# Fourteen empty GpSimd instructions in front of each indirect transfer in place of eight, in a kernel whose order of work is planned anew for it

## The chip, the cores and the metric

The kernel runs on one core of one Trainium2 chip. What is measured is the device time of one execution in microseconds, from a median over runs; profiles are of single executions. TensorE (PE) does the matmuls, PEld is its weight load, VectorE is DVE, ScalarE is ACT, GpSimd is POOL, and SyncE (SP) issues the plain transfers.

## What is computed

Two layers, one behind the other. The first mixes 8 sequences of 2496 rows of 256 numbers in the frequency domain:

```
X = rfft(x, axis=1)
Yr = Xr @ w_r - Xi @ w_i + b_r ;  Yi = Xr @ w_i + Xi @ w_r + b_i
Y  = soft threshold of Yr and of Yi at 0.01
y  = irfft(Y)                                   # 19968 rows of 256
```

The second sends each of the 19968 rows to one of 8 experts. The scores are `y @ w_gate`; all row-expert pairs are walked from the highest score down, a row takes the first expert that has room, and each expert has room for 2496 rows. A row's result is `relu(row @ w1[e]) @ w2[e]`, with 1024 hidden units.

## The kernel before

**Stages.** The sequences are worked on one after the other (batch 0 to 7). Each goes through a transform over 39 points (11 pieces), a transform over 64 points with the weights and the soft threshold (10 units, "p"), its way back (T2, lines 1153 to 1165), and the inverse transform over 39 points (11 pieces, lines 1171 to 1211), after which the rows are stored to `YD`, transposed, split in three bf16 parts (lines 1211 to 1222) and multiplied with the gate; the scores are stored to `LG`. Products that need fp32 accuracy are made of a high and a low part, so most results leave PSUM twice, once by ACT (high part) and once by DVE or POOL (the remainder).

**Routing and experts.** After half of the batches an early round gives each expert 512 rows (8 jobs of 4 row tiles). Then eight closing rounds follow, one expert each. A closing round finds its threshold by a search: DVE counts (line 454), PE adds the counts over the partitions (lines 464 and 465), DVE decides (lines 482 to 486). Then PE, ACT and DVE make the list of rows (`lists`), and the expert takes the remaining 1984 rows in 16 tiles of 128.

**Indirect transfers.** Gathers of rows (line 640), of an expert's weights (line 617) and the scatter of results (line 702) are indirect transfers that POOL issues: 32 + 128 gathers of rows, 32 of weights, 160 scatters, 352 in all. All go through one helper, and `GAP` empty instructions stand ahead of each:

```
def ind(self, pos, emit, nbytes, reads, writes, run=1024, late=0.0, bare=False):
    g = Q['gb'] if bare else Q['gw']
    def spaced():
        for _ in range(GAP): self.P.engine_nop()
        return emit()
    return self.plan.add('P', g + 1.05, pos, spaced, reads, writes, load=moved(nbytes, run, g + 1.2, 1.4, late))
```

POOL also makes the remainders of the inverse transform's input (line 955) and, for some batches, the third part of the rows (line 1222).

**The order.** Nothing is ordered by hand. Each operation is given to a planner (`Plan`) with its engine, an assumed duration, a position and what it reads and writes. The planner plays the program through with these durations and writes each engine's instructions in the order in which it could start them, with the position as the tie-break. On the chip every engine then runs its own list strictly in that order and waits where an input is late. The numbers that steer it are `Q` (positions, spacings and a few assumed costs), `LATE` (how much later than computed transfers land: `sp` plain ones, `raw` weights, `gather`, `scatter`), `SLACK` (a reserve added when an input comes from another engine), and the sets of batches that choose the engine for an operation: `BV` (the bias is added by DVE at line 1126; for other batches PE adds it with one more matmul, line 1120), `SOFT` (the soft threshold's first step runs on ACT, line 1139; for others on DVE, line 1142), `YLV` (the third part of the rows is made by DVE; for others by POOL, both line 1222). `gb` and `gw` are the cost that the planner counts for the empty instructions, `gb` for the second gather into a buffer, `gw` for all other indirect transfers.

Of the kernel before, what the change touches and what calls it, by code (L numbers as in the profile page):

```python
# [273 lines left out]
        return max(t.end for t in self.tasks)  # L274


GAP = 8
REV = True
UX = 6
P1X = -7.47  # L280
LATE = dict(sp=1.71, raw=8.75, gather=1.87, scatter=6.24)
SLACK = dict(split=1.82, count=0.02, back=0.12, lists=0.47, os=0.66, hid=0.45, mm4=0.34, mm4l=0.17, tr=0, trl=0.67, gate=0, gatel=0.55)
IOTA = True
Q = dict(hV=0.094, hA=0, hT=0, hP=0.264, e0=55.111, e1=84, en=225.161, le=33.14, ge=20.432, c0=1023.643, cs=63.758, c1=1110.092, c1a=1127.294, n0=190.708, n2=98.843, ll=30.291, gs=26.531, gl=3.929, be=16.256, bl=61.604, xp=14.084, f0=7.351, p1=0.237, p1s=0.741, p57=2.721, p57s=0.545, p5=3.525, p56s=0.982, p5s=0.706, xl=0.922, xs=0.435, m2=-0.211, m3=0.7, zz=0.824, m4=1.256, l5=0.297, s5=-1.07, w5=0.141, t5=0.888, g5=1.134, r0=16.37, gb=0.407, gw=0.319, lg=0.185, aa=0.3, ba=0.243, sc=1.967, k2=2.026)
YLV = (0, 1, 5, 7)
SOFT = (2, 3, 4, 5)


def moved(nbytes, run, lead=1.6, back=1.8, late=0.0, k=16): return lead, nbytes / run * (0.009 + 3.68e-5 * run if run <= 4096 else 7e-5 * run) / k, back + late
# [21 lines left out]
class Kit:  # L311

    def __init__(self, tc, nc, ctx, rings, groups={}):
        self.tc, self.nc = tc, nc
        self.V, self.A, self.P, self.T = nc.vector, nc.scalar, nc.gpsimd, nc.tensor
        self.plan = Plan(rings, groups, hold=dict(V=Q['hV'], A=Q['hA'], T=Q['hT'], P=Q['hP']))
        self.sp = ctx.enter_context(tc.tile_pool(name="sb", bufs=1))
# [18 lines left out]

    def dma(self, pos, emit, nbytes, reads, writes, run=1024, late=0.0, **k): return self.plan.add('SP', 0.4, pos, emit, reads, writes, load=moved(nbytes, run, late=LATE['sp'] + late), **k)
# [8 lines that stand above are left out]
# [99 lines left out]
def count(K, H, pos, c, no, ag, cols, pk, junk, acc, eqs=[], nt=1):  # L445
# [17 lines left out]
    def mm():  # L463
        T.matmul(ps.t[:, 0:n], lhsT=H.ones, rhs=cn.t[:, 0:n], start=True, stop=True)
        if n2: T.matmul(ps.t[:, n:2 * n], lhsT=H.sml, rhs=cn.t[:, n:2 * n], start=True, stop=True)
    K.t(.15, p, mm, [cn, H.b_ones, H.b_sml], [ps], slack=SLACK['count'])
    return ps
# [54 lines left out]
def lists(K, H, pos, pre, ps2, cols, nt, iota, bs, pk, jl, gi, o, top, parts, group=None):  # L522
# [10 lines left out]
    ps3 = K.psum(pk, [128, cols + 1])  # L533
    K.t(.1, pos(), lambda: T.matmul(ps3.t, lhsT=H.dif, rhs=RD.t, start=True, stop=True), [RD, H.b_dif], [ps3], slack=SLACK['lists'])
    plan.add('A', .052 + cols / 1200, pos(), lambda: A.copy(RDd.t, ps3.t), [ps3], [RDd], slack=SLACK['lists'])
    SmP = []
# [7 lines left out]
    for a, b in parts:  # L544
        for t0 in range(a, b, per):
# [3 lines left out]
            def mm(t0=t0, n=n, pl3=pl3):  # L549
                for q in range(n):  # L550
                    T.matmul(pl3.t[:, q], lhsT=Sm.t[:, 128 * (t0 + q):128 * (t0 + q) + 128], rhs=RDd.t, start=True, stop=True)
            Sm.users.append(K.t(.09 * n, pos(), mm, [RDd] + SmP[t0:t0 + n], [pl3], slack=SLACK['lists']))
            d = done[t0] = plan.buf(None, None)
# [41 lines left out]
class Experts:  # L595
# [7 lines left out]
    def load(self, pos, e=None, wi=None):  # L603
# [3 lines left out]
        for k in range(2):  # L607
            for m in range(2):
# [7 lines left out]
                else:  # L616
                    K.ind(p, lambda r=r, k=k, m=m: K.P.indirect_dma_start(out=r.t, out_offset=None, in_=self.rows[k],
                                                                          in_offset=bass.IndirectOffsetOnAxis(ap=wi.t[:, m:m + 1], axis=0)), 524e3, [wi], [r], run=4096, late=LATE['raw'])

# [10 lines left out]
    def run(self, n, base, W, gi, go, gs, oi, oo, pos_g, early=False):  # L630
# [6 lines left out]
        for t in range(NT):  # L637
            if not t % 2: xg[t // 2] = K.sb("xg", [128, 2, 256])
            g = xg[t // 2]
            q = K.ind(pos_g(t), lambda t=t, g=g: P.indirect_dma_start(  # L640
                out=g.t[:, t % 2], out_offset=None, in_=self.YD[0:EB * S] if early else self.YD, in_offset=bass.IndirectOffsetOnAxis(ap=gi.t[:, go + t:go + t + 1], axis=0)),
                131e3, [gs[t]] + (self.YDb[0:EB] if early else self.YDb), [g], late=LATE['gather'], bare=t % 2 == 1)
            gi.users.append(q)

        def xpose(c, pos):
            nt = min(4, NT - 4 * c)
            xT[c] = [[K.sb("xT", [128, 512], F32R) for _ in range(2)] for _ in range(2)]
            for m in range(2):
                h, l = xT[c][m]
                ps = K.psum("psx", [128, 512])  # L650

                def tr(ps=ps, m=m):
                    for q in range(nt):
                        t = 4 * c + q
                        T.transpose(ps.t[:, 128 * q:128 * q + 128], xg[t // 2].t[:, t % 2, 128 * m:128 * m + 128], H.idn)  # L655
                K.t(.109 * nt, pos + .5 * m, tr, [H.b_idn] + [xg[t] for t in range(2 * c, 2 * c + (nt + 1) // 2)], [ps])
                w = 128 * nt
                plan.add('A', .052 + w / 1200, pos + .5 * m, lambda ps=ps, h=h: A.copy(h.t[:, 0:w], ps.t[:, 0:w]), [ps], [h])
                v(w, pos + .5 * m, lambda ps=ps, h=h, l=l: V.tensor_tensor(l.t[:, 0:w], ps.t[:, 0:w], h.t[:, 0:w], op=OP.subtract), [ps, h], [l])

        def ffn1(c, ft, pos):
            w = min(512, n - 512 * c)
            hh, hl = K.sb("hid", [128, 512], F32R), K.sb("hid", [128, 512], F32R)
            hT[c, ft] = (hh, hl)
            ps = K.psum("psh", [128, 512])

            def mm(m):
                h, l = xT[c][m]
                for q, (a, x_) in enumerate(((0, h), (0, l), (1, h))):
                    T.matmul(ps.t[:, 0:w], lhsT=W1[m].t[:, a, 128 * ft:128 * ft + 128], rhs=x_.t[:, 0:w], start=q + m == 0, stop=q + m == 3)  # L670
            for m in range(2):
                K.t(3 * (.004 + .000446 * w), pos + .5 * m, lambda m=m: mm(m), [W1[m]] + xT[c][m], [ps])
            hi = plan.buf(None, None)
            plan.add('A', .052 + w / 1200, pos, lambda: A.activation(hh.t[:, 0:w], ps.t[:, 0:w], AF.Relu), [ps], [hh, hi])
            e = w - n % 128 if c == NC - 1 else w
            if e < w: v(w - e, pos, lambda: V.scalar_tensor_tensor(hh.t[:, w:2 * w - e], ps.t[:, e:w], 0.0, hh.t[:, e:w], op0=OP.max, op1=OP.subtract), [ps, hi], [hh])
            v(e, pos, lambda: V.scalar_tensor_tensor(hl.t[:, 0:e], ps.t[:, 0:e], 0.0, hh.t[:, 0:e], op0=OP.max, op1=OP.subtract), [ps, hi], [hl])

        def ffn2(c, q, pos):
# [21 lines left out]
            def sc():  # L701
# [3 lines left out]
                self.scat.append(ins)  # L705
            K.ind(pos + Q['sc'], sc, 131e3, [o, oi], [], late=LATE['scatter'])

        HD, k = 2, base
        xpose(0, base - Q['xp'])
        for ft in range(HD): ffn1(0, ft, base - Q['f0'] + ft)  # L710
        for c in range(NC):
# [8 lines left out]
            for q in sorted(range(min(4, NT - 4 * c)), reverse=REV and not early and c == NC - 1):  # L720
                ffn2(c, q, k)
                k += Q['k2']

# [177 lines left out]


PLAIN1, PLAIN5 = (), (7,)
BV = (0, 1, 2, 3, 4)
BANKS = [f"b{i}" for i in range(7)] + ["pt0"]
QUOTA = dict(p1=2, p5=2, ps2=2, ps3=2, pa=1, ps4=2, pT=2, pL=1, psh=3, pl=1, pso=2, psx=1, pq=1)
LATER = ('psh', 'pl', 'pso', 'psx', 'pq')
# [2 lines left out]
def phase_a(K, H, x, w_r, w_i, b_r, b_i, w_gate, cD1, cF, cG, cD5, YD, LG, NB=B):  # L910
# [26 lines left out]
    def act(n, ps=True): return (0.052 if ps else 0.095) + n / 1200  # L937
    def dve(n): return 0.068 + n / 960
# [3 lines left out]
    def add_dma(pos, emit, nbytes, reads=(), writes=(), eng='SP', after=(), run=1024, k=16, late=None):  # L942
        return plan.add(eng, 1.05 if eng == 'P' else 0.4, pos, emit, reads, writes, after=after, load=moved(nbytes, run, *((1.2, 1.4) if eng == 'P' else ()), late=LATE['sp'] if late is None else late, k=k))

# [84 lines left out]
    def batch(b):  # L1029
# [66 lines left out]
        for p in range(10):  # L1096
# [19 lines left out]

            pb = b not in BV

# [18 lines left out]
            plan.add('V', dve(512), pos + Q['zz'], lambda pc=pc, sx=sx, y=y: V.tensor_tensor(y.t, pc.t, sx.t[:, None, :].to_broadcast([128, 2, 256]), op=OP.add), [pc, sa], [y], uses=[sx])  # L1137
            if b in SOFT:
                plan.add('A', act(512, False), pos + Q['zz'], lambda y=y, t=t: A.activation(t.t, y.t, AF.Relu, bias=mlam, scale=1.0), [y, Bml], [t])
# [362 lines left out]
```

## Time and profile before

| | |
|---|---|
| Time, median of 3 runs | 1576.14 us (1571.86 to 1578.77) |
| The profiled execution's own time | 1571.82 us |
| Its span, from the first to the last instruction | 1570.0 us |
| Mean granted TensorE clock | 0.987 of full speed |
| PE busy | 1496.4 us (95%) |
| DVE busy | 1209.5 us (77%) |
| ACT busy | 883.9 us (56%) |
| POOL busy | 515.0 us (33%) |

The span begins with 47 us in which the first data arrive. To about 556 us the transforms run, with the early round's lists from about 380 us on; the last batch's scores and the experts' early jobs follow to about 790 us, and then the closing rounds' experts to the end. Busy shares are means over these stages. Matmuls are pipelined and overlap in the records, so what one more matmul costs is read from when the next ones start.

### The profile page before, as it was taken

The numbers are of one execution on the slowest core, as the hardware profiler recorded it, in microseconds if no ns is written. First come the engines' busy times: TensorE is split into PE (matmuls) and PEld (weight loads), VectorE is DVE, ScalarE is ACT, GpSimd is POOL, SyncE is SP. The second block draws the span as 40 slices with busy tenths as digits, with TensorE's granted clock in tenths as the row PEclk, the third lists the DMA queues.
The fourth block names the chain that finished last, engine by engine and source line by source line (L and its number), as shares of the span: only waits on it lengthen the run. The fifth ranks groups of instructions, "written<-read, shape, count | busy, mean of one in ns | idle before, by whom it ended". The sixth has DMA issues, their size and how long they took to land.

```text
span 1570.0 us, 31267 instructions
## 1 busy us (share of the span) xinstructions
PE 1496.4 (95%) x9391; PEld 1245.5 (79%) x9398; DVE 1209.5 (77%) x3999; ACT 883.9 (56%) x2060; POOL 515.0 (33%) x486
## 2 busy tenths in 40 slices
PE   6999999999999899998999999898999999999997
PEld 4888888888788758887787887787887878878886
DVE  5889887778999877998899997897787765563432
ACT  2778999998798854445435253344353442652331
POOL 0012215244353623114415224225233252454111
PEclk8999999999999999999999999999999999999999
DMA  9787888887788574332213122122111221231000
GB/s 323 217 275 250 245 267 273 232 268 210 239 252 251 171 206 136 110 112 92 81 44 95 33 75 63 33 76 70 63 61 52 78 70 54 92 96 61 22 24 28
DMA packets 138387, 212.07 MB, mean 135 GB/s; under 512 B 27188, under 2 KB 99553, under 8 KB 138209
## 3 DMA queue, kind: packets, MB, share of 16 engines
q1 hardware_dynamic: 118239, 151.66, 30.9%
q0 software_dynamic: 19840, 58.22, 11.7%
q8 instruction: 76, 1.25, 0.3%
q14 instruction: 102, 0.84, 0.2%
q10 hardware_dynamic: 130, 0.11, 0.0%
HBM read 125.18 MB, written 84.75 MB: 134 GB/s over the span
## 4 chain that ended last, share of the span: by engine, by line
PE 75%; DVE 13%; ACT 5%; DMA 3%; issue 2%; POOL 1%; another core or an unknown queue 1%; SPq 0%; POOLq 0%; ACTq 0%; DVEq 0%
PE b L670 21%; PE b L689 14%; PE b L690 7%; PE b L1124 6%; PE b L1153 4%; PE b L1105 3%; PE pt L670 3%; PE b L1132 3%; DVE junk L454 3%; PE b L1191 3%; PE b L1067 2%; PE pt L689 2%; PE b L655 1%; PE b L1211 1%; PE pt L690 1%
## 5 line engine op out<-in xcount | busy, mean ns | idle before, releaser
L955 POOL TENSOR_TENSOR s2l<-s2c,s2h 120x512 fp32r<-120x512 f32 (+1 forms) x84 | 105.7, 1265 | 272.4 <-ACT s2h L952 231.0
L454 DVE SCALAR_TENSOR_TENSOR junk<-h_m,st,h_AG 128x156 bf16<-128x156 f32 (+1 forms) x472 | 160.4, 382 | 2.2
L702 POOL DMA_INDIRECT out_dram<-xTh,li x64 | 65.4, 1022 | 273.4 <-DVE xTh L699 154.5
L1124 PE MATMUL b<-wt,xTh 128*128 128x256 f32 x640 | 126.6, 295 | 0.0
L1124 PEld LDWEIGHTS b<-wt,xTh 128*128 128x128 f32 x640 | 102.7, 191 | 7.5 <-issue 2.9
L1105 PE MATMUL b<-FG,sh 128*128 128x128 f32 x640 | 89.2, 281 | 12.7 <-DMA sh<-T 12.7
L702 POOL DMA_INDIRECT out_dram<-xTl,li x64 | 65.8, 1028 | 97.2 <-DVE xTl L699 64.9
L1105 PEld LDWEIGHTS b<-FG,sh 128*128 128x128 f32 x640 | 82.7, 195 | 18.3 <-DVE s2h L1008 13.6
L1124 PE MATMUL b<-wt,xTl 128*128 128x256 f32 x320 | 91.7, 287 | 2.6 <-DVE xTl L1114 2.3
L698 ACT COPY xTh<-b 128x256 f32<-128x256 f32 x62 | 23.3, 376 | 105.1 <-PE b L690 87.4
L1153 PE MATMUL b<-y,FG 64*128 64x256 f32 x640 | 80.3, 390 | 0.0
L1222 POOL TENSOR_TENSOR yTl<-yr,yTh 128x468 bf16<-128x468 f32 (+1 forms) x44 | 49.3, 1122 | 72.3 <-ACT yTh L1218 65.8
L1153 PEld LDWEIGHTS b<-y,FG 64*128 64x128 f32 x640 | 58.3, 186 | 13.4 <-issue 1.1
L1137 DVE TENSOR_TENSOR y<-b,sx 128x512 f32<-128x512 f32 x80 | 55.0, 687 | 17.6 <-ACT sx L1135 16.8
L1216 DVE TENSOR_TENSOR yr<-b,yTh 128x468 f32<-128x468 f32 (+1 forms) x85 | 52.9, 624 | 19.0 <-ACT yTh L1215 16.8
L1191 PE MATMUL b<-s2h,d 120*117 120x512 f32 (+1 forms) x168 | 66.0, 398 | 1.0 <-ACT yst L1193 0.9
L698 ACT COPY xTl<-b 128x256 f32<-128x256 f32 x71 | 26.7, 376 | 70.0 <-PE b L690 46.5
L1124 PEld LDWEIGHTS b<-wt,xTl 128*128 128x128 f32 x320 | 61.0, 190 | 4.8 <-DVE xTl L1114 4.6
L1067 PE MATMUL b<-xh,d 117*120 117x512 f32 (+1 forms) x154 | 63.8, 422 | 0.0
L1132 PE MATMUL b<-wt,xTh 128*128 128x256 f32 x320 | 63.0, 289 | 0.0
L955 DVE TENSOR_TENSOR xl<-xt,xh 117x512 fp32r<-117x512 f32 (+1 forms) x77 | 57.6, 756 | 6.6 <-ACT xh L952 6.4
L1193 ACT COPY yst<-b 117x512 f32<-117x512 f32 (+1 forms) x94 | 52.3, 559 | 10.7 <-PE b L1184 6.0
(1049 smaller groups left out, 5342.5 us busy)
## 6 DMA issues: line engine op xcount, KB each, us to landing
sh<-T SPq DMA_DIRECT2D x40, 512.0 KB
T<-s4st SPq DMA_DIRECT2D x80, 256.0 KB
s2c<-T SPq DMA_DIRECT2D x80, 240.0 KB
YD<-yst SPq DMA_DIRECT2D x80, 234.0 KB
xt<-in_x_dram SPq DMA_DIRECT2D x35, 512.0 KB
T<-s1st SPq DMA_DIRECT2D x73, 240.0 KB
xt<-in_moe_w_dram SPq DMA_DIRECT2D x32, 512.0 KB
sh<-in_x_dram SPq DMA_DIRECT2D x5, 512.0 KB
```

The costliest lines, as they stand in the source:

```text
L454: v(cols + 59, p, lambda k=k: V.scalar_tensor_tensor(junk[k % 2].t[:, 0:cols], H.m[:, 0:cols], c.t[:, k // ng:k // ng + 1], ag(k % ng)[:, ...
L670: T.matmul(ps.t[:, 0:w], lhsT=W1[m].t[:, a, 128 * ft:128 * ft + 128], rhs=x_.t[:, 0:w], start=q + m == 0, stop=q + m == 3)
L689: T.matmul(ps.t, lhsT=hh.t[:, u:u + 128], rhs=W2[ft // 4].t[:, :, ft % 4], start=ft == 0, stop=False)
L690: T.matmul(ps.t[:, 0], lhsT=hl.t[:, u:u + 128], rhs=w_[0], start=False, stop=ft == 7)
L702: ins = P.indirect_dma_start(out=self.out, out_offset=bass.IndirectOffsetOnAxis(ap=oi.t[0:M, oo + t:oo + t + 1], axis=0), in_=o.t[0:M], in ...
L955: lambda: eng.tensor_tensor(lb[1](), src(), hb[1](), op=OP.subtract), [srcb, hb[0]], [lb[0]], port=True)
L1067: T.matmul(ps.t[0:M, gs_], lhsT=d1[0:k_, a, 0:M], rhs=v.t[0:k_, gs_], start=i == 0, stop=i == 2)
L1105: T.matmul(ps.t[:, :, dt, i], lhsT=sh[k // 8].t[:, k % 8, 128 * dt:128 * dt + 128], rhs=at(Ft, k), start=True, stop=True)
L1124: T.matmul(pc.t[:, c], lhsT=a.t[:, 1 - c, dt], rhs=wt[2 - c].t[:, w, dt], start=not pb and dt == 0 and a is th and w == 0, stop=(c == 1 or ...
L1132: T.matmul(pa.t, lhsT=a.t[:, 2, dt], rhs=wt[0].t[:, w, dt], start=dt == 0 and a is th and w == 0, stop=dt == 1 and a is tl)
L1153: T.matmul(ps4[i].t[:, r], lhsT=at(Gt, 2 * (p - 1 + r) + c)[h], rhs=zs[r].t[h, c], start=c == 0, stop=c == 1)
L1191: T.matmul(ps.t[0:M, gs_], lhsT=d5[0:k_, a, 0:M], rhs=v.t[0:k_, gs_], start=i == 0, stop=i == 2)
```

## The change

Each indirect transfer gets 14 empty instructions in place of 8. The planner's cost for them goes from 0.407 us (`gb`) and 0.319 us (`gw`) to 0.7 and 0.71. Other numbers of the plan are changed as well: three of the four sets of batches, most reserves, and 23 of the positions, spacings and costs in `Q`. The matmuls of the experts, the tiles and the transfers stay as they are, save for the operations that the sets move between engines.

```diff
-GAP = 8
+GAP = 14
-LATE = dict(sp=1.71, raw=8.75, gather=1.87, scatter=6.24)
-SLACK = dict(split=1.82, count=0.02, back=0.12, lists=0.47, os=0.66, hid=0.45, mm4=0.34, mm4l=0.17, tr=0, trl=0.67, gate=0, gatel=0.55)
+LATE = dict(sp=1.71, raw=7.61, gather=2.51, scatter=6.24)
+SLACK = dict(split=1.92, count=0, back=0.12, lists=0.46, os=0.13, hid=0.53, mm4=0.34, mm4l=0, tr=0, trl=0.78, gate=0, gatel=0.77)
-Q = dict(... hP=0.264, e0=55.111, ... le=33.14, ... cs=63.758, c1=1110.092, c1a=1127.294, ... n2=98.843, ll=30.291, gs=26.531, ... p57=2.721, ... p56s=0.982, ... xl=0.922, xs=0.435, ... m4=1.256, l5=0.297, ... w5=0.141, ... r0=16.37, gb=0.407, gw=0.319, lg=0.185, aa=0.3, ba=0.243, sc=1.967, ...)
+Q = dict(... hP=0.251, e0=52.817, ... le=33.647, ... cs=63.442, c1=1110.327, c1a=1132.512, ... n2=111.85, ll=26.558, gs=26.411, ... p57=2.591, ... p56s=0.948, ... xl=1.223, xs=0.576, ... m4=1.384, l5=-0.434, ... w5=0.616, ... r0=14.763, gb=0.7, gw=0.71, lg=1.028, aa=0.287, ba=0.062, sc=2, ...)
-YLV = (0, 1, 5, 7)
-SOFT = (2, 3, 4, 5)
+YLV = (1, 5, 7)
+SOFT = (2, 3, 4, 5, 6)
-BV = (0, 1, 2, 3, 4)
+BV = (0, 2, 3, 4)
```

So batch 1 gets its bias from PE (10 matmuls more) and no longer from DVE (10 additions fewer), batch 0's third parts go from DVE to POOL (11 operations), and batch 6's threshold step goes from DVE to ACT (10 operations). Among the changed positions, `le` is that of the early jobs' weight loads (on SP) and `ll` of the closing rounds' (indirect, on POOL), `l5` and `w5` are those of the inverse transform's loads and of its stores, `lg` of the stores of the scores (all three on SP), `r0` and `e0` of the early routing, `c1`, `c1a`, `cs` and `n2` of the closing rounds.

## Rows read from the trace of the kernel before

**Rows 1.** The page's first part: busy us (share) and instructions, by engine.
```profile
PE 1496.4 (95%) x9391; PEld 1245.5 (79%) x9398; DVE 1209.5 (77%) x3999; ACT 883.9 (56%) x2060; POOL 515.0 (33%) x486
```

**Rows 2.** Windows: stretch, length, busy (count) of PE, PEld, DVE, ACT, POOL; clock, DMA.
```profile
47.00:330.00 283.00, 281.57 (x2216) 243.34 (x2215) 234.19 (x424) 246.52 (x545) 76.38 (x62) 1.00 0.83 257
330.00:556.00 226.00, 214.70 (x1749) 181.38 (x1754) 201.85 (x520) 190.10 (x475) 102.03 (x88) 1.00 0.73 228
556.00:790.00 234.00, 223.13 (x1227) 175.71 (x1226) 199.83 (x778) 113.50 (x244) 65.25 (x63) 0.98 0.38 117
790.00:1500.00 710.00, 683.89 (x3728) 570.40 (x3727) 523.14 (x2151) 299.43 (x732) 258.51 (x256) 0.99 0.20 63
```

**Rows 3.** Waits of PE: who waited for whom, us in total, times, longest.
```profile
PE b L464 <- DVE cnt L459: 13.7, 8, 4.7
```

**Rows 4.** Windows around PE's longest wait of the closing rounds.
```profile
984.90:989.50 4.60, 0.00 (x0) 0.00 (x0) 4.57 (x20) 1.69 (x4) 1.99 (x2) 0.84 0.08 29
989.50:995.00 5.50, 5.46 (x15) 4.30 (x16) 3.49 (x14) 1.20 (x2) 0.95 (x1) 0.51 0.16 51
```

**Rows 5.** Timeline of POOL, sixth closing round: start, us, what [idle before <-releaser].
```profile
1263.26 0.95 POOL L640 DMA_INDIRECT xh<-YD,li  x1 [0.40 <-issue]
...
1270.86 0.94 POOL L702 DMA_INDIRECT out_dram<-xTh,li  x1 [3.95 <-DVE xTh L696]
1272.21 1.03 POOL L702 DMA_INDIRECT out_dram<-xTl,li  x1 [0.41 <-DVE jl L515]
...
1276.47 0.99 POOL L640 DMA_INDIRECT s2h<-YD,li  x1 [0.41 <-issue]
1278.38 0.96 POOL L640 DMA_INDIRECT yTh<-YD,li  x1 [0.92 <-issue]
```

**Rows 6.** Line 343 in 842.240 to 842.380 us: count, ns minimum/median/maximum, first and last start.
```profile
L343 POOLq ENGINE_NOP  x7: 32/32/32, 842.2 to 842.4; - x7
```

**Rows 7.** Lines 640 and 702: POOL's idle time before them until this released them (us, times).
```profile
  issue: 57.8, 127
...
  DVE xTh L699: 226.0, 43
...
  issue: 12.2, 22
```

**Rows 8.** Timeline of PE around one bias matmul of batch 5: start, us, what.
```profile
374.18 0.38 PE L1120 MATMUL b<-bb,h_ones 128*128 128x512 bf16 x1
...
374.64 0.28 PE L1124 MATMUL b<-wt,xTl 128*128 128x256 f32 x1
374.76 0.40 PE L1124 MATMUL b<-wt,xTh 128*128 128x256 f32 x2
374.99 0.28 PE L1124 MATMUL b<-wt,xTl 128*128 128x256 f32 x1
```

**Rows 9.** Windows over batch 1's and batch 6's units, columns as in the second group.
```profile
90.00:152.00 62.00, 61.56 (x486) 52.96 (x485) 56.54 (x111) 52.20 (x117) 15.35 (x12) 1.00 0.80 251
410.00:475.00 65.00, 63.73 (x507) 53.32 (x507) 60.90 (x172) 56.58 (x148) 26.33 (x22) 1.00 0.81 251
```

**Rows 10.** Operations that change engine: count, ns minimum/median/maximum, first and last start.
```profile
L1126 DVE TENSOR_TENSOR b<-b,bf x50: 684/693/700, 33.6 to 332.9; 128x512 f32<-128x512 f32 x50
L1222 DVE TENSOR_TENSOR yTl<-yr,yTh x44: 473/639/1225, 113.5 to 586.1; 128x468 bf16<-128x468 f32 x40, 128x312 bf16<-128x312 f32 x4
L1222 POOL TENSOR_TENSOR yTl<-yr,yTh x44: 787/1088/2230, 237.5 to 556.2; 128x468 bf16<-128x468 f32 x40, 128x312 bf16<-128x312 f32 x4
L1142 DVE TENSOR_SCALAR y<-y x40: 408/426/1496, 35.3 to 541.5; 128x512 f32<-128x512 f32 x40
L1139 ACT ACTIVATE y<-y,ml x40: 721/726/805, 151.4 to 408.6; 128x512 f32<-128x512 f32 x40
```

**Rows 11.** PE's second transposes of that closing round; DMA busy tenths, 1258 to 1262 us.
```profile
1280.78 0.38 PE L655 MATMUL b<-h_idn,s2h 128*128 128x128 f32 x2
...
DMA  0000000000000000000000000000597837000020
```

More of the change, by code (lines that the diff above doesn't have):

```diff
@@ L280 @@
 P1X = -7.47
-LATE = dict(sp=1.71, raw=8.75, gather=1.87, scatter=6.24)
-SLACK = dict(split=1.82, count=0.02, back=0.12, lists=0.47, os=0.66, hid=0.45, mm4=0.34, mm4l=0.17, tr=0, trl=0.67, gate=0, gatel=0.55)
+LATE = dict(sp=1.71, raw=7.61, gather=2.51, scatter=6.24)
+SLACK = dict(split=1.92, count=0, back=0.12, lists=0.46, os=0.13, hid=0.53, mm4=0.34, mm4l=0, tr=0, trl=0.78, gate=0, gatel=0.77)
 IOTA = True
-Q = dict(hV=0.094, hA=0, hT=0, hP=0.264, e0=55.111, e1=84, en=225.161, le=33.14, ge=20.432, c0=1023.643, cs=63.758, c1=1110.092, c1a=1127.294, n0=190.708, n2=98.843, ll=30.291, gs=26.531, gl=3.929, be=16.256, bl=61.604, xp=14.084, f0=7.351, p1=0.237, p1s=0.741, p57=2.721, p57s=0.545, p5=3.525, p56s=0.982, p5s=0.706, xl=0.922, xs=0.435, m2=-0.211, m3=0.7, zz=0.824, m4=1.256, l5=0.297, s5=-1.07, w5=0.141, t5=0.888, g5=1.134, r0=16.37, gb=0.407, gw=0.319, lg=0.185, aa=0.3, ba=0.243, sc=1.967, k2=2.026)
-YLV = (0, 1, 5, 7)
-SOFT = (2, 3, 4, 5)
+Q = dict(hV=0.094, hA=0, hT=0, hP=0.251, e0=52.817, e1=84, en=225.161, le=33.647, ge=20.432, c0=1023.643, cs=63.442, c1=1110.327, c1a=1132.512, n0=190.708, n2=111.85, ll=26.558, gs=26.411, gl=3.929, be=16.256, bl=61.604, xp=14.084, f0=7.351, p1=0.237, p1s=0.741, p57=2.591, p57s=0.545, p5=3.525, p56s=0.948, p5s=0.706, xl=1.223, xs=0.576, m2=-0.211, m3=0.7, zz=0.824, m4=1.384, l5=-0.434, s5=-1.07, w5=0.616, t5=0.888, g5=1.134, r0=14.763, gb=0.7, gw=0.71, lg=1.028, aa=0.287, ba=0.062, sc=2, k2=2.026)
+YLV = (1, 5, 7)
+SOFT = (2, 3, 4, 5, 6)
 def moved(nbytes, run, lead=1.6, back=1.8, late=0.0, k=16): return lead, nbytes / run * (0.009 + 3.68e-5 * run if run <= 4096 else 7e-5 * run) / k, back + late
```

## The prediction

> **What bounds the kernel now.** I read the page's first part, then the windows by stage, then PE's waits, and only then POOL's timeline. The page says that PE is busy for 1496.4 of 1570.0 us and POOL for 515.0 [rows 1]; the reader is to see that POOL, the engine that the change lengthens, has two thirds of its time free. A share over the whole span can hide a stage with another limit, so the windows come next [rows 2]. From 47 to 330 us PE is idle for 283.00 - 281.57 = 1.4 us: that stage is PE's alone. From 330 to 556 us it is idle for 11.3 us, from 556 to 790 for 10.9, and through seven of the closing rounds, 790 to 1500 us, for 26.1. Together 49.7 us, and no other engine comes near its stretch's length there, so what PE waits for is single inputs that come late and not an engine at its bound. The largest family is the matmul that adds the search's counts (line 464) and waits for DVE: 13.7 us in 8 waits, the longest 4.7 [rows 3]. Since PE runs its list strictly in order, the expert's matmuls behind such a wait stand still too, though their inputs are there. A long wait costs a second time: after 4.60 us without a matmul the granted clock is 0.51 for the next 5.5 us, about the lower of its two levels (1.2 of 2.4 GHz), so some 0.49 x 5.5 = 2.7 us of work are lost behind it [rows 4].
>
> The sum is made against the profiled execution's own time, 1571.8 us (1.8 more than its span). It is the low end of the three runs; their median, 1576.1, lies 4.3 higher.
>
> **The empty instructions themselves.** In 0.14 us seven of them start, one per 0.02 us [rows 6]. Six more for each of 352 transfers are 2112 x 0.02 = 42 us of POOL's time if all of it counts. From below they cost nothing; from above the whole pause of 0.41 us between two transfers [rows 5] is theirs, 0.41 / 8 = 0.05 each and 0.31 us per transfer. I take 0.02, so 0.12 us, because that is the nearest row: eight of them fill only 0.16 us of the pause of 0.41. They count only where POOL goes from one transfer straight to the next. Most scatters wait for a result: 226.0 us of POOL's idle time ahead of line 702 end on DVE's sum at line 699, in 43 waits [rows 7], and the empty instructions, which wait for nothing themselves, pass before that. Straight behind another transfer come 127 gathers of rows and 22 scatters, together 149 [rows 7], so about 149 x 0.12 = 18 us of POOL are added, over 1100 us in which it is idle for two thirds.
>
> Who waits for POOL? A scatter only has its buffer and the end behind it; for a gather PE's transposes wait. In the sixth closing round the second set of transposes needs a gather that POOL began at 1276.47 [rows 5], and PE reads it at 1280.78 [rows 11]. A gather begun at 1259.14 moves its data until about 2.4 us later: in 40 slices of 0.1 us the DMA row is busy until the 34th, 1261.4 us [rows 11]. So that gather is there at 1278.9 and has 1.9 us to spare. Since POOL's last wait for a result, at 1270.86, four pauses lie before it, which makes it 4 x 0.12 = 0.5 us later, at the upper bound 4 x 0.31 = 1.2. Both are below 1.9: cost on the path 0.
>
> The Trainium skill bears on this in the page "Runtime: NRT & Kernel Launch", section "Instruction fetch mechanics": instructions are loaded in blocks ahead of use and the load hides behind the sequencer's own pace. By it six more instructions cost only their own 0.12 us. The trace does not quite agree: one pause between two gathers is 0.92 us where its neighbours are 0.41 [rows 5], on "issue", with nothing that it waits for. If that is such a load, more instructions bring more of them; one more in the four pauses above makes 0.5 + 0.5 = 1.0 us, still below 1.9.
>
> **The bias of batch 1.** PE gets 10 matmuls of 128x512 bf16. From the bias matmul's start to the third matmul behind it are 374.64 - 374.18 = 0.46 us, the same two without it take 374.99 - 374.76 = 0.23 [rows 8]; one costs 0.23 us, ten cost 2.3. In batch 1's stretch PE is busy for 61.56 of 62.00 us [rows 9], so nothing covers it: at least 2.3 - 0.4 = 1.9 us, at most 10 x 0.38 (its recorded duration) = 3.8. I take +2.3. DVE saves 10 x 0.69 = 6.9 us [rows 10], which buys at most the 0.4 us that PE is idle there.
>
> **Batch 0's third parts** leave DVE (11 x 0.64 = 7.0 us) for POOL (11 x 1.09 = 12.0 us), which works for 15.35 us in those 62 [rows 9, 10]. The room is there. The trace shows what POOL does to DVE at such times: the threshold step of line 1142 takes 0.43 us as a rule and up to 1.50 [rows 10]. If each of batch 1's ten steps were hit, DVE would lose 10.7 us, and 56.5 - 6.9 - 7.0 + 10.7 = 53.3 is still below the 62: value 0, between 0 and -0.4. The Trainium skill's page "SBUF — State Buffer", section on who interferes with whom, speaks against this edit: a DVE instruction with two SBUF inputs or in a doubled mode and a GpSimd instruction that reads SBUF shut each other out. The spread of line 1142 agrees; by the sum just made it is hidden.
>
> **Batch 6's threshold** takes 10 x 0.43 = 4.3 us from DVE and gives 10 x 0.73 = 7.3 to ACT. ACT is then busy for 56.6 + 7.3 = 63.9 of 65 us, as long as PE with 63.7 [rows 9, 10]. That is the tightest place: if ACT ends late there, PSUM comes free late, and I allow +2. The gain is at most PE's idle time of 1.3 us. Value 0.
>
> **The new order.** The other edits are assumed costs, reserves and positions. None adds work, but all lists come out anew: of SP (loads of the inverse transform later by `l5`, stores of scores by `lg`), of POOL (gathers and the closing rounds' weights, later by `ll`, between scatters) and of PE, DVE and ACT. So the 49.7 us of waits and the time lost to the clock are drawn again. Two facts say how. The planner counted 1.05 + 0.41 = 1.46 us per gather or 1.37 where the chip takes 1.36 (0.95 + 0.41 [rows 5]); now it counts 1.75 where about 1.48 are to be expected. It will think gathers later than they are, eight in a row by 2 us, and so put their transposes further back on PE: safe, and not needed. And the waits that cost most, of the count matmul, hang on how well the planner knows DVE, of which the durations are unchanged. I see no reason for fewer or more: value 0, from -17 (a third of the 49.7 goes) to +14 (below).
>
> The sum: 1571.8 + 2.3 = 1574.1 on the profiled execution's level, 1578.4 on the median's. I give 1575.
>
> **The rivals.**
> *The new order takes out long waits.* The counts' 13.7 us end because DVE's searches and PE's list fit better, and three or four stretches at half the clock like that in rows 4 go with them. For it: eight waits make up all of the 13.7, so a few changed places are enough. Against it: the planner learns nothing new of DVE. 1574 - 13.7 - 2.7 = 1558.
> *Gathers come late (the other side).* If POOL's bursts grow by more than the 1.9 us that the second transposes have to spare, PE stands in front of them, in each of the five rounds whose gathers run just ahead of PE. It decides from 1.9 us later: at 0.12 per pause that takes 15 pauses in a row, at 0.31 six. Each such wait of about 1 us plus some half-speed time behind it, like the 2.7 us of rows 4 at most, makes up to 5 x 2.8 = 14 us: 1588. For it: 16 gathers and as many scatters share POOL's list in a round. Against it: the planner counts even more than the chip will take.
> *The empty instructions do nothing.* If the pause is set by the next transfer's own start and not by them, it stays 0.41, and only the plan changes: also 1574.
>
> **Chances and range.** My forecast, with or without longer pauses, has 0.49, with a spread of some 6 us for waits drawn again; its own range is 1567 to 1583. Fewer waits has 0.30, late gathers 0.18, the rest lies farther out. The range of 1556 to 1591 takes in the two rivals' times. What a measurement can tell from no change is about 0.5%, 8 us. Of the forecast's 0.49 some 0.37 lie within it, 0.09 above and 0.03 below; of fewer waits 0.26 are faster; late gathers are slower in 0.15. So faster 0.30, no change 0.45, slower 0.25.
>
> **What would show it.** In the changed kernel's POOL timeline the pauses read 0.53 us (0.41: the empty instructions are hidden; 0.7: they are dearer). Line 1120 has ten more matmuls, the first near 95 us, and everything behind batch 1 starts some 2 us later. PE's waits in the windows from 330 to 1500 us sum to 40 to 60 us, the most still of line 464 on DVE. A gap of line 655 on a gather would bear out late gathers. The prediction is wrong if the waits sum to less than 35 us, or if the stretch to 330 us gets shorter.

## The result, and the profile after

The changed kernel takes 1535.43 us (median of 4 runs, 1534.72 to 1537.15), the kernel before in the same measurement 1577.04 (1571.86 to 1578.77). The ratio is 0.9737, with a 95% interval of 0.9714 to 0.9759: 42 us faster, where the forecast was 1575 and the range ended at 1556.

The profiled execution took 1537.15 us, with a span of 1535.3 and a mean granted clock of 0.993 (0.987 before). Its page begins, as in [rows 1]:

```profile
PE 1487.0 (97%) x9398; PEld 1239.6 (81%) x9408; DVE 1195.0 (78%) x3968; ACT 890.9 (58%) x2070; POOL 528.8 (34%) x497
```

PE is busy for 9.4 us less, and its idle time falls from 1570.0 - 1496.4 = 73.6 to 1535.3 - 1487.0 = 48.3, by 25.3. Together these are the 34.7 us between the two spans. The windows of [rows 2] say where (stretch, length, busy and count of PE, PEld, DVE, ACT, POOL; clock, DMA):

```profile
47.00:330.00 283.00, 281.95 (x2218) 244.28 (x2222) 225.74 (x401) 245.57 (x542) 90.13 (x72) 1.00 0.82 255
330.00:556.00 226.00, 211.77 (x1726) 177.70 (x1729) 195.01 (x497) 191.72 (x477) 95.91 (x84) 0.99 0.72 225
556.00:790.00 234.00, 228.74 (x1282) 179.47 (x1275) 207.71 (x800) 118.51 (x257) 72.52 (x68) 1.00 0.40 124
790.00:1500.00 710.00, 707.57 (x3894) 594.79 (x3893) 531.31 (x2169) 313.39 (x752) 261.70 (x260) 1.00 0.20 64
```

In the closing rounds PE idles for 2.4 us in place of 26.1, from 556 to 790 for 5.3 in place of 10.9, from 330 to 556 for 14.2 in place of 11.3: 21.9 in place of 49.7. PE's waits from 330 us on (who waited for whom, us in total, times, longest), which answer to [rows 3]:

```profile
PE b L1153 <- DVE y L1143: 3.6, 3, 1.9
PE b L1124 <- DVE xTl L1114: 2.2, 3, 1.7
PE b L464 <- DVE cnt L459: 2.2, 5, 0.8
PE pt L464 <- DVE cnt L459: 2.1, 3, 1.1
```

The count matmul's wait (into `b`) falls from 13.7 us, at most 4.7 at once, to 2.2, at most 0.8. The closing rounds' stretches at half the clock [rows 4] are gone; one is left ahead of them, behind 2 us with next to no matmul:

```profile
521.00:523.00 2.00, 0.08 (x4) 0.04 (x2) 2.00 (x4) 0.25 (x1) 0.89 (x1) 1.00 0.25 66
523.00:526.50 3.50, 3.50 (x13) 2.02 (x13) 3.50 (x9) 2.54 (x5) 1.42 (x2) 0.52 0.28 83
```

POOL's timeline in the sixth closing round, to be read against [rows 5]:

```profile
1226.54 1.00 POOL L640 DMA_INDIRECT xh<-YD,li  x1 [0.54 <-issue]
1228.44 1.01 POOL L702 DMA_INDIRECT out_dram<-xTl,li  x1 [0.90 <-issue]
...
1238.92 0.95 POOL L640 DMA_INDIRECT xl<-YD,li  x1 [0.53 <-issue]
```

The pause is 0.53 us where 0.41 stood, as forecast; but between about two thirds of the transfers that follow one another (160 of the 243 pauses below 0.95 us) it is 0.75 to 0.95, which was not. By the empty instructions alone that isn't plain: in both kinds of pause the 14 start within 0.3 us (0.02 each, as in [rows 6]), here ahead of the transfers of 1226.54 and of 1230.28, whose pauses are 0.54 and 0.84.

```profile
L343 POOLq ENGINE_NOP  x14: 59/59/59, 1226.0 to 1226.3; - x14
L343 POOLq ENGINE_NOP  x14: 80/80/80, 1229.4 to 1229.7; - x14
```

Read so far, the rival "the new order takes out long waits" seems to have won, and by more than it promised. The runs say something else.

**What the stops of the kernel before look like.** One stretch of its sixth closing round, all engines:

```profile
1286.61 0.95 POOL L640 DMA_INDIRECT s2l<-YD,li  x1 [0.40 <-issue]
...
1286.87 0.39 PE L670 MATMUL b<-yTh,sh 128*128 128x512 f32 x1
1288.60 0.17 DVE L482 TENSOR_REDUCE g<-b 128x3 f32<-128x6 f32 x1 [1.56 <-remote]
1288.65 0.60 ACT L674 ACTIVATE xh<-b 128x512 fp32r<-128x512 f32 x1 [2.33 <-remote]
1288.80 0.16 DVE L483 TENSOR_SCALAR_CACHE_REDUCE g<-g 128x3 f32<-128x3 f32 x1
1288.81 0.95 POOL L640 DMA_INDIRECT y<-YD,li  x1 [1.25 <-remote]
```

For 1.7 us PE, DVE and ACT start nothing, and POOL, whose transfer ended at 1287.56, stands in front of the next; then DVE, ACT and POOL go on within 0.21 us, and PE after them. It is not one engine that the others wait for. Such stretches, of more than 0.5 us without a start on PE, DVE and ACT (their sequencers' own instructions counted as starts), are 16 between 737 and 1500 us in the kernel before (11.0 us in all); in the changed kernel there is none. The count is a rough sign only: in twelve of the 16 an operation that began earlier is still running, and a run that loses nothing in this way (the longer sums on chip E, below) has nine. Stretches of more than 0.2 us in which nothing at all runs on the three engines are 4 in the kernel before (3.0 us) and none in the changed one.

**What is late are the signals.** A stop need not bring every engine to a stand. The longest wait of [rows 4] begins like this, in the kernel before and then, for the same instructions, in the same program on a chip without the loss (chip A below):

```profile
977.39 0.17 PE L465 MATMUL b<-cnt,h_sml 128*128 128x9 bf16 x1
978.42 0.38 PE L655 MATMUL b<-h_idn,xl 128*128 128x128 f32 x2
980.07 0.18 DVE L482 TENSOR_REDUCE g<-b 128x3 f32<-128x18 f32 x1 [2.44 <-PE b L655]
981.98 0.95 POOL L640 DMA_INDIRECT s4st<-YD,li  x1 [0.40 <-issue]
983.75 0.59 ACT L658 CAST s1st<-b 128x512 fp32r<-128x512 f32 x1 [7.04 <-PE b L670]
```

```profile
966.24 0.17 PE L465 MATMUL b<-cnt,h_sml 128*128 128x9 bf16 x1
966.45 0.18 DVE L482 TENSOR_REDUCE g<-b 128x3 f32<-128x18 f32 x1 [0.19 <-PE b L465]
967.27 0.38 PE L655 MATMUL b<-h_idn,xl 128*128 128x128 f32 x2
967.68 0.59 ACT L658 CAST s1st<-b 128x512 fp32r<-128x512 f32 x1 [2.31 <-PE b L655]
```

DVE's step starts 2.5 us after PE's sum has ended, where the other chip has 0.04; ACT's cast starts 5.0 us after its transposes, where the other has 0.03, and 0.8 us after the end of GpSimd's row of transfers. The trace's records of PE's signals agree: the one for the sum, which ended at 977.56, stands at 980.04, and six that belong to operations ended by 982.73 stand together between 983.70 and 984.02; on the other chip such a record stands 0.01 to 0.02 us behind the end. PE itself went on to 984.8 with the work that it had in hand, and only then stood for 4.7 us. That wait is booked on DVE, which was busy for 4.57 of 4.60 us of it [rows 4] with what had reached it late.

### The profile page after: what moved, and what is told of

Same layout as the page of the kernel before. It is cut to its first block, busy times and chain, and to the rows that moved or that the text cites. A ratio compares the mean times of both kernels' runs of the same rounds, so it can differ in the third digit from the quotient of the medians.

```text
span 1535.3 us, 33346 instructions
## 1 busy us (share of the span) xinstructions
PE 1487.0 (97%) x9398; PEld 1239.6 (81%) x9408; DVE 1195.0 (78%) x3968; ACT 890.9 (58%) x2070; POOL 528.8 (34%) x497
## 4 chain that ended last, share of the span: by engine, by line
PE 75%; DVE 12%; DMA 5%; ACT 4%; issue 3%; SPq 1%; POOL 0%; POOLq 0%; DVEq 0%; ACTq 0%
PE b L670 21%; PE b L689 15%; PE b L690 8%; PE b L1124 5%; PE b L1153 3%; PE b L1105 3%; PE pt L670 3%; PE b L1067 3%; PE b L1132 3%; PE b L1191 2%; DVE junk L454 2%; DMA s2c<-T 2%; PE b L655 2%; PE pt L689 2%; PE b L1211 1%
## 5 line engine op out<-in xcount | busy, mean ns | idle before, releaser
L1222 POOL TENSOR_TENSOR yTl<-yr,yTh 128x468 bf16<-128x468 f32 (+1 forms) x55 | 64.6, 1176 | 91.4 <-ACT yTh L1218 86.3
L699 DVE TENSOR_TENSOR xTl<-b,xTl 128x256 f32<-128x256 f32 x74 | 31.2, 421 | 51.2 <-ACT xTl L698 46.9
L1191 PE MATMUL b<-s2h,d 120*117 120x512 f32 (+2 forms) x166 | 65.8, 402 | 0.1
L617 POOL DMA_INDIRECT xt<-in_moe_w_dram,wi x32 | 32.8, 1024 | 89.0 <-DVE sh L627 31.2
```

The lines of the kernel that those rows point to most:

```text
L1191: T.matmul(ps.t[0:M, gs_], lhsT=d5[0:k_, a, 0:M], rhs=v.t[0:k_, gs_], start=i == 0, stop=i == 2)
```

## The experiments

All variants differ from one of the two kernels by a line or two. "Order before" and "new order" are the schedules of the kernel before and of the changed one. The runs were taken on five chips, and the kernel before ran beside each: it took 1532.3 to 1533.9 us on three of them (A: 1533.9 and 1533.5; C: 1532.7; E: 1532.3) and 1569.3 and 1575.8 on the others (B and D), as it did (1577.0) where the result was measured. Times are medians in us.

| | empty instructions | where before takes 1532 to 1534 | where before takes 1569 to 1577 |
|---|---|---|---|
| order before | 0 | 1531.16 (A), 1530.25 (C) | 1596.80 (D) |
| | 8 (the kernel before) | 1533.87 (A), 1532.74 (C) | 1569.28 (B), 1575.80 (D) |
| | 11 | 1532.86 (C) | 1549.73 (D) |
| | 14 | 1534.62 (A), 1534.55 (E) | 1535.70 (B) |
| new order | 0 | 1537.30 (A), 1536.37 (C) | 1562.79 (D) |
| | 8 | 1535.98 (A) | 1548.20 (B) |
| | 14 (the changed kernel) | | 1534.02 (B), 1535.43 (result) |

### On chip A: no count of empty instructions does anything

The new order with 8:

```diff
-GAP = 14
+GAP = 8
```

> The changed kernel's order on every engine, kept as it is, with 8 empty instructions ahead of each indirect transfer instead of 14. If the new order alone brings the gain (the count matmuls' waits are gone because the lists fit better), it stays at 1535 us or gets some 0 to 3 us faster, and PE's waits from 790 us on stay near 2 us. If the empty instructions bring it (with eight, GpSimd's pauses of 0.7 us inside the row of empty instructions come back, and PE's waits with them), it goes back to 1560 to 1577 us.

Measured: 1.0015 [1.0005, 1.0025] of the kernel before. The order before with 14:

```diff
-GAP = 8
+GAP = 14
```

> The kernel before, its order on every engine as it is, with 14 empty instructions instead of 8. By the order theory it stays at 1577 us, give or take 5, with PE's waits from 790 us on near 26 us. By the theory that the empty instructions matter it comes down to 1540 to 1555 us; gathers planned for the shorter pauses may then cost a few us.

Measured: 1.0007 [0.9996, 1.0017]. Neither half of the change gains anything here. The new order without any (`GAP = 0`), and with 14 that the planner counts at the old price:

> The changed kernel's order with no empty instruction at all. By the order theory 1535 us or a little less, since GpSimd only gets ahead. If the empty instructions keep something from happening, this is the worst of all: 1580 us or more, with more of the waits that nothing in the profile explains.

Measured: 1.0020 [1.0010, 1.0030].

```diff
-Q = dict(... gb=0.7, gw=0.71, ...)
+Q = dict(... gb=0.407, gw=0.319, ...)
```

> The changed kernel with 14 empty instructions, but planned with the old cost for them (0.407 and 0.319 us instead of 0.7 and 0.71); the order is planned anew with all other new numbers. If the counted cost is what made the order good, the waits return: 1555 to 1577 us. If the other numbers or the empty instructions on the chip did it, 1535 to 1545 us.

Measured: 1.0017 [1.0006, 1.0029]. Then the order before without any, and the kernel before unchanged with a profile of its own:

> The kernel before, its order as it is, with no empty instruction at all. If the time of the kernel before is set by the place where it runs (a chip on which signals stop for some 0.7 us at a time during bursts of gathers, or one on which they don't), this stays within 4 us of the kernel before on the same chip: near 1534 us on a chip without the stops; on a chip with them 1577 or more. If empty instructions are what keeps the stops away, it is 1577 us or more on every chip.

> The kernel before, unchanged, for its profile on this chip. If the stops belong to the chip: on a chip where it takes 1534 us no pause of 0.7 us stands inside a row of empty instructions, and PE's waits from 790 us on are below 4 us; on one where it takes 1577 us some 16 such pauses and 26 us of waits. If its own order made the waits, they are there on every chip, and its time is 1577 us.

Measured: 0.9986 [0.9973, 0.9999] and 0.9996 [0.9981, 1.0011]. The profile of the unchanged kernel on this chip is the key. Its page and its windows:

```profile
PE 1486.4 (97%) x9398; PEld 1241.2 (81%) x9398; DVE 1211.8 (79%) x3999; ACT 885.3 (58%) x2060; POOL 515.1 (34%) x486
```

```profile
330.00:556.00 226.00, 214.21 (x1739) 180.55 (x1739) 201.31 (x514) 188.94 (x473) 99.80 (x86) 0.98 0.73 224
556.00:790.00 234.00, 227.82 (x1273) 179.55 (x1272) 207.73 (x808) 117.00 (x250) 67.73 (x66) 1.00 0.40 122
790.00:1500.00 710.00, 707.58 (x3897) 595.53 (x3896) 533.42 (x2155) 311.50 (x752) 264.27 (x261) 1.00 0.21 64
```

The same program idles on PE for 11.8 + 6.2 + 2.4 = 20.4 us from 330 us on, where [rows 2] have 49.7. So the 26.1 us of waits in the closing rounds were not this schedule's: where nothing stops, the order before already has the waits of the new one (21.9).

### On chip B: the loss is there, and 14 empty instructions end it in either order

The changed kernel unchanged, and the first two edits once more.

> The changed kernel unchanged, beside the kernel before on the same chip. If the 42 us belong to the two kernels themselves: 1535 us against 1577, a ratio near 0.974. If they belong to the place at which the kernel before was profiled (semaphore signals held up in its gather bursts): where the kernel before takes about 1534 us the changed one takes 1536 to 1537, a ratio of 1.0015 to 1.002, which is the 2.3 us of ten more bias matmuls; where the kernel before takes about 1577 the changed one takes 1535 again.

> The changed order with 8 empty instructions in front of each indirect transfer in place of 14, once more. Where the kernel before takes about 1534 us: 1536, as in the first run of this kernel. Where the kernel before takes about 1577 us: if the longer row of empty instructions is what keeps the signals moving, 1565 to 1580 us; if it is the new order, 1535.

> The order before with 14 empty instructions in place of 8, once more. Where the kernel before takes about 1534 us: 1534.6, as in the first run of this kernel. Where it takes about 1577 us: if the longer row of empty instructions is what keeps the signals moving, 1534 to 1540 us; if it is the new order, 1565 to 1580.

Measured, against 1569.28: 0.9761 [0.9728, 0.9795], 0.9856 [0.9823, 0.9890] and 0.9769 [0.9735, 0.9803]. The longer row of empty instructions gives all of the gain to the order before, which is otherwise untouched; the new order alone gives 21 of the 35 us, which lies between the two times expected of it (1565 to 1580, or 1535). The gains don't add up: with 14 there is nothing left for the order to save.

### On chips C and D: none, 11, and the new order with none

`GAP = 0` and `GAP = 11` with the order before, `GAP = 0` with the new one; first on chip C, where the kernel before takes 1532.7 us:

> The order before without any empty instruction. If what holds the signals up is that transfers follow each other too closely (the pause between two transfers then falls from 0.41 to 0.24 us): where the kernel before takes about 1570 us, 1575 to 1620 us. If it is the short row of empty instructions itself in which GpSimd stops: no row, no stop, 1531 to 1540 us. Where the kernel before takes about 1534 us: 1531, as in the first run of this kernel, which tells neither.

> The order before with 11 empty instructions in place of 8. If the loss follows the pause between transfers (0.47 us with 11, between 0.41 and 0.53): 1545 to 1560 us where the kernel before takes about 1570. If a part of the pauses grows to 0.7 us and more, as with 14, and that is what is needed: 1534 to 1540 us. Where the kernel before takes about 1534 us: 1534.

> The new order without any empty instruction. If too close transfers lose the time: where the kernel before takes about 1570 us, above the 1548 us that the new order takes there with 8 empty instructions, 1550 to 1590. If it is the row of empty instructions itself: 1536 to 1540. If the new order spreads the transfers enough by itself: 1537, as where the kernel before takes 1534 us.

Measured: 0.9992 [0.9977, 1.0006], 1.0005 [0.9992, 1.0018], 1.0026 [1.0015, 1.0038]. Nothing is lost, so nothing is told apart. Then on chip D, where it takes 1575.8:

> The order before without any empty instruction, once more, for a chip on which the kernel before takes 1569 us or more. If the transfers follow each other too closely there: 1575 to 1620 us. If the short rows of empty instructions themselves lose the time: 1531 to 1540 us. Where the kernel before takes about 1533 us: 1530, as twice before.

> The order before with 11 empty instructions, once more (on a chip where the kernel before took 1533 us, its pauses were 0.47 us, without the longer ones that 14 bring). Where the kernel before takes 1569 us or more: 1545 to 1560 us if the loss falls with the pause; 1560 to 1575 if only the longer pauses of 14 help. Where the kernel before takes about 1533 us: 1533.

> The new order without any empty instruction, once more. Where the kernel before takes 1569 us or more: 1550 to 1590 us if too close transfers lose the time; 1536 to 1540 if the short rows of empty instructions do. Where the kernel before takes about 1533 us: 1536, as before.

Measured: 1.0122 [1.0081, 1.0164], 0.9824 [0.9780, 0.9868], 0.9910 [0.9880, 0.9940]. Fewer is worse: 1597, 1576, 1550 for 0, 8 and 11, and 1536 on B for 14, with pauses between two gathers of 0.30, 0.41, 0.47, and 0.53 or 0.8. So the theory that the short rows of empty instructions themselves lose the time falls (without any, the kernel should have taken 1531 to 1540), and the one that transfers follow one another too closely stands. The 61 us between 0 and 14 come from two chips, but each stands against the kernel before on its own.

Two profiles of the same program tell the loss without any count of stops. ACT's instructions are the same, one by one; the table has how much later the one stands that the undisturbed profile (chip A or C) has at 737 us and at 1450 us:

| | empty instructions | late on, against | at 737 us | at 1450 us |
|---|---|---|---|---|
| order before | 0 | D, C | 5.8 | 67.8 |
| | 8 | place of [rows 1], A | -4.3 | 38.0 |
| | 11 | D, C | 0.9 | 15.6 |
| | 14 | B, A | 1.0 | 1.2 |
| new order | 0 | D, C | -0.6 | 24.3 |
| | 8 | B, A | 0.9 | 12.9 |

Nearly all of the loss arises between these two times, it falls from none to 8, 11 and 14 empty instructions, and with 14 nothing of it is left.

The run without any makes the best picture, since the same program was profiled on both chips. The window of 790 to 1500 us, on C and then on D:

```profile
790.00:1500.00 710.00, 707.39 (x3894) 595.33 (x3894) 531.81 (x2137) 311.06 (x751) 266.50 (x263) 1.00 0.21 64
```

```profile
790.00:1500.00 710.00, 670.01 (x3612) 558.32 (x3611) 518.38 (x2156) 292.56 (x717) 254.09 (x251) 0.97 0.20 62
```

On D PE idles there for 40.0 us in place of 2.6. One of the 26 stretches without a start, in the timeline of D:

```profile
765.76 0.95 POOL L640 DMA_INDIRECT sh<-YD,li  x1 [0.30 <-issue]
...
765.95 0.39 PE L689 MATMUL b<-FG,s1st 128*128 128x512 f32 x1
767.01 0.95 POOL L640 DMA_INDIRECT y<-YD,li  x1 [0.30 <-issue]
768.26 0.95 POOL L640 DMA_INDIRECT y<-YD,li  x1 [0.30 <-issue]
770.02 0.17 DVE L503 TENSOR_SCALAR_CACHE_REDUCE g<-b 128x7 f32<-128x7 f32 x1 [6.34 <-remote]
...
771.10 0.58 PE L690 MATMUL b<-FG,s2h 128*128 128x256 f32 x1 [4.76 <-DVE st L504]
```

GpSimd runs transfer after transfer with 0.30 us between them. In the 4.1 us from 765.95 to 770.02 PE, DVE and ACT start nothing at all, and they come back 0.8 us after the last transfer has ended. PE's wait is then booked on DVE, which had been standing still itself. The clock pays a second time, as in [rows 4]: in the stretch with this stop it is 0.95 in the mean and behind it 0.50, the lower of its two levels (1.2 of 2.4 GHz).

```profile
762.00:770.00 8.00, 3.44 (x20) 2.71 (x20) 1.03 (x4) 0.60 (x1) 5.67 (x6) 0.95 0.35 102
770.00:776.10 6.10, 4.80 (x15) 3.85 (x16) 6.05 (x27) 3.15 (x6) 0.00 (x0) 0.50 0.07 21
```

Over the whole run: the span grows from 1528.5 on C to 1596.5 on D, by 68.0, PE's busy time from 1484.5 to 1506.3 by the lower clock, so 21.8 of the 68.0 are clock and 46.2 are idle time.

What the stops are not, these two profiles show as well. Their queue of loaded instructions (packets, MB, share of 16 engines) reads the same on both chips, and so does the queue of the indirect transfers apart from the share (12.1% on C, 11.7% on D, of a longer span):

```profile
q0 software_dynamic: 19840, 58.22, 11.7%
...
q14 instruction: 80, 0.66, 0.1%
```

Neither the loading of instructions nor slower transfers make the difference. By the Trainium skill's page "Runtime: NRT & Kernel Launch", section "Instruction fetch mechanics", such loads are mostly hidden; these two traces show only that they are not what differs.

One thing in the records does differ, and it marks the place even where no time is lost. By the profiles of A, each of the 352 transfers raises its semaphore 16 times, 5632 updates in all. The twelve profiles from A, C and E hold 99.7 to 99.9% of them, the eight from B, D and the place of the result 55 to 70%, the changed kernel's own 68%. The list of transfers shows it (C, then D): the last number, the time in us from issue to landing, can be told on C alone.

```profile
xh<-YD,li POOLq DMA_INDIRECT x14, 2.8
```

```profile
xh<-YD,li POOLq DMA_INDIRECT x14
```

Why the new order loses less with the same pause (1548 against 1569 with 8, 1563 against 1597 with none): counted on chips A and C, where nothing stops, the order before sends up to 36 transfers in a row with pauses below 0.45 us after 730 us (8 empty instructions; 29 with none), the new order at most 10 (9 with none). It plans 1.75 us for a gather, so scatters and other work fall between. That fits the stops: on D, without any, 26 stretches without a start of more than 0.5 us between 737 and 1500 us (31.2 us) in the order before, 8 (5.2 us) in the new one; with nothing running at all on PE, DVE and ACT, 14 (19.5 us) and 2 (1.0 us). No run changes the length of these rows alone.

### On chip E: time between transfers, or a number of instructions?

Two kernels put one sum on GpSimd in place of the empty instructions:

```diff
-            for _ in range(GAP): self.P.engine_nop()
+            if pos > 900: self.P.tensor_tensor(self.bf[:, 0, 32:64], self.bf[:, 0, 0:32], self.bf[:, 0, 0:32], op=OP.add)
```

the second 128 numbers wide in place of 32; the third is `range(14 if pos > 900 else 0)`. The condition turned out to hold for all 352 transfers, not for the closing rounds' alone, so the third is again the order before with 14.

> The order before without empty instructions; ahead of each indirect transfer of the early stages nothing, of the closing rounds one small sum on GpSimd (128x32 numbers of a tile that is no longer needed). If what counts is the time between two transfers: with a pause of 0.45 to 0.6 us, 1533 to 1555 us where the kernel before takes 1569 us or more. If it is the number of instructions in between: one is like none, 1580 to 1600. Where the kernel before takes about 1533 us: 1530 to 1534.

> As the one ahead of it, with a longer sum (128x128 numbers), so that the pause is 0.7 us or more. If the time between two transfers counts: 1531 to 1540 us where the kernel before takes 1569 us or more, at or below the shorter sum. If the number of instructions counts: 1580 to 1600. Where the kernel before takes about 1533 us: 1530 to 1538.

> The order before with 14 empty instructions ahead of the closing rounds' indirect transfers and none ahead of the earlier ones. If the loss arises in the closing rounds alone: 1532 to 1537 us where the kernel before takes 1569 us or more. If the earlier gathers lose time too: 1540 to 1550. Where the kernel before takes about 1533 us: 1531 to 1535.

Measured, where the kernel before takes 1532.3: 1.0032 [1.0018, 1.0046], 1.0192 [1.0173, 1.0211] and 1.0015 [1.0006, 1.0025]. There was nothing to lose on this chip, so the question stays open. The pauses came out at 0.43 and 0.60 us (medians of those below 1.1), shorter than the 0.45 to 0.6 and 0.7 that were meant. The first missed its expectation of 1530 to 1534 by 3 us, the second its 1530 to 1538 by 23 us, for a reason of its own:

```profile
PE b L464 <- DVE cnt L459: 14.7, 15, 3.2
```

These are PE's waits in the closing rounds from 790 us on (4.3 us with the shorter sum). GpSimd's 352 sums of 0.4 us lengthen DVE's counts (line 454: mean 423 ns; 381 in the third kernel, with 14 empty instructions), and the count matmul waits for them. From 330 to 1500 us PE idles for 43.5 us in place of the third kernel's 20.9, which makes 22.6 of the 24.5 us between their spans. The Trainium skill's page "SBUF — State Buffer", section "Who interferes with whom", names one pair of ports that DVE and GpSimd share; the 423 against 381 ns agree with it.

## Why the prediction was wrong

**The failed step is the price of the empty instructions.** In "The empty instructions themselves" I bounded it by nothing from below and by 0.31 us per transfer from above and put its cost on the path at 0. The words "from below they cost nothing" shut out a gain with no reason given. They had one: 1569.28 - 1535.70 = 33.6 us with the order before on chip B, where the rows of transfers hold up the signals between the engines and longer pauses end that. The row that hinted at it was there: the pause of 0.92 us "on issue" in [rows 5], which I took for a load of instructions if it was anything, and asked only what more of them would cost. Its eight empty instructions take 0.7 us from the first start to the last, those of the 0.41 us pause ahead of it 0.2:

```profile
L343 POOLq ENGINE_NOP  x8: 11/42/42, 1277.4 to 1278.1; - x8
L343 POOLq ENGINE_NOP  x8: 68/68/68, 1276.0 to 1276.2; - x8
```

On chip A the same program's same pause is 0.41:

```profile
1249.98 0.96 POOL L640 DMA_INDIRECT yTh<-YD,li  x1 [0.41 <-issue]
```

So the pause was not the program's. That what holds GpSimd up inside it is the same thing that makes the signals late is likely, but no run shows it by itself.

**The waits drawn again.** I took 49.7 us of PE's waits and 13.7 of the count matmul's as the schedule's own, gave a new schedule no reason for fewer, and put this term at 0. The changed kernel has 21.9, below the 35 that I had named as the sign of being wrong, and line 464 still has the most of it, as forecast (2.2 and 2.1 us). But the unchanged kernel has 20.4 on chip A. The other 29.3 us are there only where the signals come late; with the clock (PE busy 1496.4 against 1486.4, 10.0 us), less 1.2 in the other stretches, they are the 38.1 us between the two spans of the same program, 1570.0 and 1531.9. They were booked on whichever signal came last, mostly DVE's counts.

**Rivals.** The time fell as in "takes out long waits", whose price of 16 us was less than half, but its mechanism isn't the one shown: on chip A the new order takes out nothing, and the 21 us that it takes out on chip B with 8 are of the hold-ups. The price was also short by its own words: three or four stretches at half the clock are 8 to 11 us and not 2.7, which gives 1549 to 1552, below the range's end. "Gathers come late" did not happen: PE is never idle in front of line 655 in the profile after. The 1.9 us of room were read too large: on chip A the gathers of that buffer land 2.8 us after their issue and not 2.4, which leaves 1.5, still above the 1.2 of the upper bound.

```profile
s2h<-YD,li POOLq DMA_INDIRECT x6, 2.8
```

"The empty instructions do nothing" is wrong on both counts, pause and time.

**What held.** A third of the pauses read 0.53 us. The other edits cost a few us where nothing stops: the new order is 2.1 us slower than the order before at 8 empty instructions (1535.98 against 1533.87) and 6.1 at none (1537.30 against 1531.16). The bias of batch 1 was forecast at +2.3; the trace of before and after shows less:

```profile
L1120 PE MATMUL b<-bb,h_ones x30: 376/381/500, 85.9 to 544.2; 128*128 128x512 bf16 x30
```

```profile
L1126 DVE TENSOR_TENSOR b<-b,bf x40: 685/692/700, 34.4 to 334.8; 128x512 f32<-128x512 f32 x40
```

The first line is a group with 30 of the 40 matmuls (their weight loads are 40 in place of 30). They begin at 85.9 us where about 95 was forecast. Line 1126's first addition is 0.8 us later than in [rows 10], its last, behind batch 1, 1.9: so 1.1 us were added in between, less than the forecast's lower end of 1.9. The 0.4 us of PE's idle time in batch 1's stretch [rows 9] were used up:

```profile
90.00:152.00 62.00, 61.99 (x489) 53.56 (x489) 48.57 (x90) 51.36 (x115) 28.41 (x22) 1.00 0.81 250
410.00:475.00 65.00, 62.75 (x500) 52.60 (x502) 55.06 (x164) 57.34 (x154) 20.81 (x19) 1.00 0.78 247
```

Batch 0's thirds on POOL are hidden there, as forecast. In batch 6's stretch PE idles for 2.25 us in place of 1.27, within the 2 allowed.

**What stays open.** What decides whether the signals come late at a place (two of five chips, and the place of the result); each chip but A was seen in one stretch of time only, so chip and moment are not told apart. By what path transfers of GpSimd hold up the other engines' signals. Whether time between transfers or the number of instructions counts, and why most pauses with 14 are 0.75 us and more. One rival is untested: all executions here were recorded by the profiler (each has a span and a granted clock), and where time is lost the records have holes, so the recording itself may take part; no run without it is there. The changed kernel itself was not run on a chip without the loss, so its time there (1536 to 1537 expected) is not known.

## What to carry to other kernels

Before a wait is priced as a schedule's own, hold it against a second profile of the same program on another chip, instruction by instruction: here 29.3 of 49.7 us of waits were not the schedule's. Within one trace, look for stretches in which no engine runs anything and all go on at once, and for steps that start long after the operation that they wait for has ended; the releaser that is named need not be what was late. Where GpSimd sends indirect transfers one behind the other, longer pauses between them can be worth more than the time they take (34 us on chip B), but what fills them matters: fourteen empty instructions in place of eight cost 0.8 and 2.3 us on chips A and E, sums of 128x128 numbers 29 on E.

## What the runs showed of the hardware

- While indirect transfers follow one another by 0.30 to 0.47 us, signals between the engines come late on some chips and not on others, for the same program: 2.5 and 5.0 us in the example of the kernel before, 0.04 and 0.03 on chip A, with up to 5.7 us without a start on PE, DVE and ACT on D. The time is 1596.80 us on D, 1530.25 on C.
- On the places with the loss 30 to 45% of the records of the transfers' semaphore updates are missing, on the others 0.1 to 0.3%, also for kernels that lose no time.
- Empty instructions on GpSimd start every 0.02 us. Pauses between two transfers are 0.30 us with none, 0.41 with 8, 0.47 with 11: the first eight add 0.11 us, the next three 0.06. With 14 they are 0.53 or, in two thirds of the cases, 0.75 to 0.95.
- A sum of 128x128 numbers on GpSimd ahead of each transfer, 0.42 us each, costs the whole kernel 29 us (1561.38 against 1532.3), mostly by way of DVE's counts.
